# When weights are converted and inner-layer sums are split in the attention half of an attention and mixer kernel

## The chip, the core and the metric

The kernel runs on one core of a Trainium2 chip. The metric is the device time of one execution in microseconds (us): 847.35 as the median of three runs of the kernel before (846.75 to 847.96).

## What is computed

```python
scores = scale * np.matmul(q, k.transpose(0, 1, 3, 2))
mask = (rel >= 0) & (rel < window)
scores = np.where(mask, scores, -1000000000.0)
attn = softmax(scores)
x = concat_heads(np.matmul(attn, v))
xt = x.transpose(0, 2, 1)
h = np.maximum(xt @ w_tok1, 0.0) @ w_tok2
u = x + h.transpose(0, 2, 1)
h2 = np.maximum(u @ w_ch1, 0.0) @ w_ch2
return (u + h2).astype(np.float32)
```

Eight batches of eight heads, 576 tokens, 64 columns a head, a window of 64 tokens. The token layers go 576 to 256 to 576 (w_tok1, w_tok2), the channel layers 512 to 1536 to 512 (w_ch1, w_ch2). The weights come as float64, and every product is made with float32 numbers split into a rounded high part and a low rest, as three matmuls (high by high, high by low, low by high).

## The kernel before

The attention half runs over 36 tiles (two blocks of 64 tokens each; nine tiles make two batches). The loop `for i in range(-1, NT + 1)` is written out as a software pipeline, and every engine does its instructions in the order in which the loop's body issues them: nothing reorders them. "Tile i" below is the stretch in which step i of this loop runs. In it, in TensorE's order:

- `pt_transpose(i, 0)` and `(i, 1)`: the exponentials of tile i (e, two halves u of four heads) are transposed (pp, L311); ScalarE copies the result to SBUF (pt, L313).
- `run_pieces`: up to two pieces of the second token layer (`tok2`, up, L403 and L410), from tile 7 on; ScalarE copies each out (u, L415) before the next can use the one bank.
- `tok1(n)`: the first token layer (h, L368) for the tile before; it needs that tile's x split into xhi (ScalarE, L101) and xlo (GpSimd, L104). The fifth tile of a pair of batches, x4, x13 and so on, is split by halves (L348, L349).
- `av(i, pts)`: probabilities by v (xp, L323).
- `qk(i + 2)`: scores two tiles ahead (s, L276). For the first seven tiles (`N_PE = 7`) TensorE adds the mask (L270), and ScalarE takes the exponentials from PSUM.

VectorE has, per tile: the maxima of tile i+1 by halves (L290 and L291 in tiles below 7, otherwise the mask and scale into e, L293, and the maximum, L296), the reciprocal of the sums (ri, L331 and L332), and the normalisation of tile i (x, L337). ScalarE has eight exponentials per tile (L304).

Two kinds of work are put between these:

- A **weight job** turns one piece of the float64 weights into float32 and splits it. `job_convert_a` is three VectorE operations (L195, L197, L198), `job_convert_b` three more (L207, L209, L210) and a GpSimd addition (w, L212). `job_finish`, one tile later, is a ScalarE cast (t1hi, t2hi or w1hi, L101) and a subtraction (L104): on GpSimd for w_tok1 (t1lo) and w_ch1 (w1lo), on VectorE for w_tok2 (t2lo). `JOBS[i]` says whether tile i converts a piece: tiles -1 to 5, then two of three. 27 pieces are done in this half; jobs 4, 5 and 6 are w_tok2.
- `finish_h(b)`, the **inner-layer split**: when a batch's h is summed up (in tiles 5, 9, 14, 18, 23, ...), ScalarE takes its relu (hhi, L379), VectorE the low rest (hlo, L380). h has two PSUM banks, so the next batch's first h matmul waits until hlo has read the bank.

The channel half (from about 265 us) is matmuls over the token chunks, with Strassen-like products in its larger part; the change issues nothing else there.

Of the kernel before, what the change touches and what calls it, by code (L numbers as in the profile page):

```python
# [26 lines left out]
TPP = 9  # L27
NT = NPAIR * TPP
# [11 lines left out]
N_FIRST = 27  # L40


JOBS = {i: 1 if i < 6 or i % 3 else 0 for i in range(-1, 37)}
PIECES = {32: (1, 0), 33: (1, 0), 34: (1, 0), 35: (3, 0), 36: (2, 1)}

TOK1_FROM, TOK1_SLOW, TOK2_FROM = 2, 4, 7
# [1 line left out]
N_PE, N_EARLY = 7, 4  # L48
# [35 lines left out]
def mixer_kernel(ctx: ExitStack, tc: tile.TileContext, qh, kh, vh, wt1, wt2, wc1, wc2, out):  # L84
# [14 lines left out]
    def split(eng_hi, eng_lo, hi, lo, src):  # L99
        if eng_hi is nc.scalar:  # L100
            nc.scalar.copy(hi, src)  # L101
        else:
            eng_hi.tensor_copy(hi, src)
        eng_lo.tensor_sub(lo, src, hi.bitcast(F32))  # L104
# [18 lines left out]
    with ExitStack() as actx:  # L123
# [21 lines left out]
        def load_v(i):  # L145
            vt = pq.tile([P, 2, H, D], F32, name=f"v{i}", tag="v", bufs=3)
            nc.sync.dma_start(vt, vh[i])
            loaded[i][1] = vt
# [71 lines left out]
        to_load, to_convert, to_finish = list(range(N_FIRST)), [], []  # L220
# [23 lines left out]
        def job_finish():  # L244
            if to_finish:
                n, w = to_finish.pop(0)
                finished.add(n)
                src, hi, lo, o, m = jobs[n]
                if hi is None:
                    nc.sync.dma_start(w2_dram[:, o:o + m], w)  # L250
                else:
                    eng = nc.vector if src is wt2 or n >= N_FIRST else nc.gpsimd
                    split(nc.scalar, eng, hi[:, o:o + m], lo[:, o:o + m], w)
                    if src is wt1 and o + m == 5 * DT:
                        for c, r in enumerate((top, bottom)):
                            nc.gpsimd.tensor_copy(t1z[r, c], t1lo[r, 4 * DT:].bitcast(F32))
# [41 lines left out]
        def softmax_exp(i, u):  # L298
            e = e_sb[i, u]
            nm, sm = st[i]  # L300
            src, by = (s_ps.pop((i, u)), scale) if i < N_PE else (e, 1.0)
            for h in range(4):
                g = 2 * h + u
                nc.scalar.activation(e[:, h], src[:, h], AF.Exp, bias=nm[:, g:g + 1], scale=by,  # L304
                                     accum_out=sm[:, g:g + 1])
# [36 lines left out]
        def split_x(i):  # L342
            xhi = pa.tile([P, C], F32R, name=f"xhi{i}", tag="xhi", bufs=NX)
            xlo = pa.tile([P, C], F32R, name=f"xlo{i}", tag="xlo", bufs=NX)
            if i % TPP == 4:

                for t, own, other in ((xhi, top, bottom), (xlo, bottom, top)):
                    nc.scalar.copy(t[own], xs[i][own])  # L348
                    nc.gpsimd.tensor_sub(t[other], xs[i][own], t[own].bitcast(F32))  # L349
            else:  # L350
                split(nc.scalar, nc.gpsimd, xhi, xlo, xs[i])
            xhl[i] = (xhi, xlo)
# [3 lines left out]
        def tok1_part(i, b, rows, slot, first, last):  # L356
            xhi, xlo = xhl[i]
            if first:
                h_ps[b] = [ps.tile([P, C], F32, name=f"h{b}_{tt}", tag="h") for tt in range(NTT)]
            for tt in range(NTT):  # L360
                if rows is full:
                    combos = ((t1hi, xhi), (t1hi, xlo), (t1lo, xhi))
                else:
                    x = xhi if rows is top else xlo
                    combos = ((t1hi, x), (None, x))
                for n, (w, x) in enumerate(combos):
                    w, o = (t1z[:, rows is bottom], 0) if w is None else (w, slot * DT)
                    nc.tensor.matmul(h_ps[b][tt], w[:, o + tt * P:o + (tt + 1) * P], x,  # L368
                                     start=first and n == 0, stop=last and n == len(combos) - 1)

        pieces, up_tags = [], [("up", 1)]

        def finish_h(b):
            hh = []
            for tt in range(NTT):
                hp = h_ps[b][tt]
                hi = pa.tile([P, C], F32R, name=f"hhi{b}_{tt}", tag=f"hhi{tt}", bufs=2)
                lo = pa.tile([P, C], F32R, name=f"hlo{b}_{tt}", tag=f"hlo{tt}", bufs=2)
                nc.scalar.activation(hi, hp, AF.Relu)  # L379
                nc.vector.scalar_tensor_tensor(out=lo, in0=hp, scalar=0.0, in1=hi.bitcast(F32),  # L380
                                               op0=ALU.max, op1=ALU.subtract)
                hh.append((hi, lo))
            h_ps.pop(b)
            for half in range(2):
                for ct in range(NCT):
                    pieces.append((b, half, ct, hh))
# [46 lines left out]
        def tok1(i):  # L433
            p, t = divmod(i, TPP)
            b0, b1 = 2 * p, 2 * p + 1
            if t < 4:
                tok1_part(i, b0, full, t, t == 0, False)
            elif t == 4:
                tok1_part(i, b0, top, 4, False, True)
                finish_h(b0)  # L440
            else:
                if t == 5:
                    tok1_part(i - 1, b1, bottom, 4, True, False)
                tok1_part(i, b1, full, t - 5, False, t == 8)
                if t == 8:
                    finish_h(b1)

        def run_pieces(k):
            for _ in range(min(k, len(pieces))):
                tok2(*pieces.pop(0))  # L450
# [21 lines left out]
        for i in range(-1, NT + 1):  # L472
            if 0 <= i and i + 2 < NT:
                load_v(i + 2)
            if 3 <= i + 3 < NT:
                load_q(i + 3)
            if i + 4 < NT:
                load_k(i + 4)
            store_u()
            n_jobs = JOBS[i]  # L480
            if i == NT - 1:
                up_tags += [("s", 2), ("pt", 2)]
            have = len(pieces)
            n_pieces = PIECES.get(i, (1, 1) if i >= TOK2_FROM else (0, 0))
            pts = []
            early = i < N_EARLY
            if 0 <= i < NT:
                pts.append(pt_transpose(i, 0))
                if i < NT - 1:
                    pts.append(pt_transpose(i, 1))  # L490
            if i + 1 < NT:
                softmax(i + 1, 0)
            if early and i > 0:
                norm(*normed.pop())
            if 0 <= i < NT:
                ri = recip(i)
            while to_finish:
                job_finish()
            for n in tok1_plan.get(i + 1, ()):
                last_use = n - NX + ((n - NX) % TPP == 4)  # L500
                if n < i and last_use not in tok1_plan.get(i, ()):
                    split_x(n)
            if i + 1 < NT:
                softmax_exp(i + 1, 0)
            run_pieces(min(have, n_pieces[0]))
            have = min(have, len(pieces))
            if not early:
                for _ in range(n_jobs):
                    job_convert_a()
            if i == NT - 1:  # L510
                pts.append(pt_transpose(i, 1))
            if i + 1 < NT:
                softmax(i + 1, 1)
            if early:
                for _ in range(n_jobs):
                    job_convert_a()
            for n in tok1_plan.get(i, ()):
                tok1(n)
            if i + 1 < NT:
                softmax_exp(i + 1, 1)  # L520
            for _ in range(n_jobs):
                job_convert_b()
            if 0 <= i < NT:
                xp = av(i, pts)
                if i + 1 < N_EARLY:
                    normed = [(i, xp, ri)]
                else:
                    norm(i, xp, ri)
            if i + 2 < NT:
                qk(i + 2)  # L530
            for n in tok1_plan.get(i + 1, ()):
                if n not in xhl:
                    split_x(n)
            run_pieces(min(have, n_pieces[1]))
            while to_load and len(to_convert) < 2 and i < NT - 2:
                job_load()
            if i == NT - 1:
                while to_convert or to_convert_b or to_finish:
                    job_convert_a()
                    job_convert_b()  # L540
                    job_finish()
                qctx.close()
                pu = uctx.enter_context(tc.tile_pool(name="pu", bufs=1, side="right", reuse_waits="tile"))
                ul = {0: load_u(0, pu)}
# [396 lines left out]
```

## Time and profile before

| what | value |
|---|---|
| median of three runs | 847.35 us |
| the profiled execution | 847.25 us, its span 845.5 us |
| TensorE busy with matmuls | 817.7 us of the span |
| VectorE, ScalarE, GpSimd busy | 527.6, 338.9, 103.1 us |
| mean granted TensorE clock | 0.998 of full speed |

The span is the time from the first to the last instruction of the profiled execution; 1.75 us lie around it. A matmul's busy time is its own, so neighbours overlap; what counts for the time is where TensorE sits idle, and what ended each such wait.

### The profile page before, as it was taken

The numbers are of one execution on the slowest core, as the hardware profiler recorded it, in microseconds if no ns is written. First come the engines' busy times: TensorE is split into PE (matmuls) and PEld (weight loads), VectorE is DVE, ScalarE is ACT, GpSimd is POOL, SyncE is SP. The second block draws the span as 40 slices with busy tenths as digits, with TensorE's granted clock in tenths as the row PEclk, the third lists the DMA queues.
The fourth block names the chain that finished last, engine by engine and source line by source line (L and its number), as shares of the span: only waits on it lengthen the run. The fifth ranks groups of instructions, "written<-read, shape, count | busy, mean of one in ns | idle before, by whom it ended". The sixth has DMA issues, their size and how long they took to land.

```text
span 845.5 us, 14791 instructions
## 1 busy us (share of the span) xinstructions
PE 817.7 (97%) x5864; PEld 680.1 (80%) x5864; DVE 527.6 (62%) x939; ACT 338.9 (40%) x1018; POOL 103.1 (12%) x109
## 2 busy tenths in 40 slices
PE   6889999999999999999999999999999999999998
PEld 4668878878879878888888888888888878888886
DVE  4989888888885697567415535366635367625252
ACT  4778889889885341213203211123202033202020
POOL 3533343343332000000000000000000000000000
PEclk9999999999999999999999999999999999999999
DMA  9657677677634545745322652424542424542002
GB/s 320 217 182 254 202 238 250 220 232 248 209 132 151 156 149 169 223 137 155 120 93 78 244 227 77 147 88 137 187 187 88 136 88 163 170 178 88 1 0 100
DMA packets 71333, 136.10 MB, mean 161 GB/s; under 512 B 7008, under 2 KB 41568, under 8 KB 69344
## 3 DMA queue, kind: packets, MB, share of 16 engines
q1 hardware_dynamic: 69152, 133.32, 46.6%
q10 hardware_dynamic: 2112, 1.84, 0.7%
q8 instruction: 46, 0.75, 0.4%
q14 instruction: 23, 0.19, 0.1%
HBM read 104.46 MB, written 30.67 MB: 160 GB/s over the span
## 4 chain that ended last, share of the span: by engine, by line
PE 74%; DVE 19%; ACT 2%; issue 2%; DMA 1%; POOL 1%; POOLq 0%; SPq 0%; DVEq 0%; ACTq 0%
PE gp L840 18%; PE op L628 11%; PE gp L620 8%; PE op_4a L628 4%; PE op_2b L628 4%; PE op_2a L628 4%; PE op_0b L628 4%; PE op_0a L628 4%; PE op_4b L628 4%; PE h L368 3%; PE up L410 3%; PE s L276 3%; PE xp L323 2%; DVE nm L296 2%; DVE e L293 2%
## 5 line engine op out<-in xcount | busy, mean ns | idle before, releaser
L840 PE MATMUL gp<-m,w1hi 128*128 128x512 f32 x504 | 155.4, 390 | 0.7 <-DVE x L848 0.7
L840 PEld LDWEIGHTS gp<-m,w1hi 128*128 128x128 f32 x504 | 94.5, 188 | 21.0 <-DVE x L848 1.5
L840 PE MATMUL gp<-m,w1lo 128*128 128x512 f32 x252 | 98.1, 389 | 0.0
L304 ACT ACTIVATE e<-e,nm 128x128 f32<-128x128 f32 x232 | 90.6, 398 | 9.1 <-DVE nm L296 9.0
L607 ACT ACTIVATE ghi<-x 128x512 fp32r<-128x512 f32 x54 | 34.1, 632 | 119.9 <-DVE x L850 68.3
L844 ACT COPY x<-gp 128x512 f32<-128x512 f32 x18 | 10.4, 577 | 143.3 <-PE gp L840 143.3
L608 DVE SCALAR_TENSOR_TENSOR glo<-x,ghi 128x512 fp32r<-128x512 f32 x54 | 37.4, 692 | 38.1 <-ACT ghi L607 38.1
L607 ACT ACTIVATE ghi<-gp 128x512 fp32r<-128x512 f32 x50 | 29.8, 597 | 67.7 <-PE gp L620 67.7
L620 PE MATMUL gp<-uhi,w1hi 128*128 128x512 f32 x144 | 56.0, 389 | 0.0
L620 PE MATMUL gp<-ulo,w1hi 128*128 128x512 f32 x144 | 56.0, 389 | 0.0
L620 PE MATMUL gp<-uhi,w1lo 128*128 128x512 f32 x144 | 56.0, 389 | 0.0
L840 PEld LDWEIGHTS gp<-m,w1lo 128*128 128x128 f32 x252 | 47.3, 188 | 9.9
L608 DVE SCALAR_TENSOR_TENSOR glo<-gp,ghi 128x512 fp32r<-128x512 f32 x50 | 34.3, 687 | 25.4 <-ACT ghi L607 25.3
L628 PE MATMUL op<-ghi,w2hi 128*128 128x512 f32 x128 | 49.8, 389 | 0.0
L628 PE MATMUL op<-ghi,w2lo 128*128 128x512 f32 x128 | 49.8, 389 | 0.0
L628 PE MATMUL op<-glo,w2hi 128*128 128x512 f32 x128 | 49.8, 389 | 0.0
L276 PE MATMUL s<-k,q 64*64 64x128 f32 x1152 | 44.7, 284 | 4.7 <-DVE c L207 2.5
L323 PEld LDWEIGHTS xp<-v,pt 128*64 128x64 f32 x1152 | 37.2, 140 | 13.7 <-issue 7.2
L104 POOL TENSOR_TENSOR xlo<-x,xhi 128x512 fp32r<-128x512 f32 x32 | 41.2, 1286 | 41.0 <-ACT xhi L101 40.6
L304 ACT ACTIVATION_READ_ACCUMULATOR e<-e,nm 128x1 f32 x232 | 45.1, 194 | 0.0
L410 PE MATMUL up<-t2hi,hhi 128*128 128x320 f32 (+1 forms) x128 | 43.0, 336 | 0.0
L323 PE MATMUL xp<-v,pt 128*64 128x64 f32 x1152 | 42.1, 227 | 0.8 <-ACT pt L313 0.6
(165 smaller groups left out, 1881.8 us busy)
## 6 DMA issues: line engine op xcount, KB each, us to landing
v<-vh SPq DMA_DIRECT2D x36, 512.0 KB, 3.9
w1hi<-w1s SPq DMA_DIRECT2D x18, 896.0 KB, 4.8
w1lo<-w1s SPq DMA_DIRECT2D x18, 896.0 KB, 6.6
raw<-wc SPq DMA_DIRECT2D x32, 384.0 KB, 4.3
q<-qh SPq DMA_DIRECT2D x36, 256.0 KB, 4.6
k<-kh SPq DMA_DIRECT2D x7, 1280.0 KB, 7.5
out<-uf SPq DMA_DIRECT2D x35, 256.0 KB, 2.6
uf<-u_dram SPq DMA_DIRECT2D x8, 1024.0 KB, 8.7
```

What stands on the lines that cost most here:

```text
L104: eng_lo.tensor_sub(lo, src, hi.bitcast(F32))
L276: nc.tensor.matmul(s[u][half * BLK:(half + 1) * BLK, j], qt[r, j, half], kbs[b][r, j, n * BLK:n * BLK + P], start=not on_pe, stop=True, sk ...
L293: nc.vector.scalar_tensor_tensor(out=e, in0=s_ps.pop((i, u)), scalar=scale, in1=mk.unsqueeze(1).to_broadcast([P, 4, P]), op0=ALU.mult, op1 ...
L304: nc.scalar.activation(e[:, h], src[:, h], AF.Exp, bias=nm[:, g:g + 1], scale=by, accum_out=sm[:, g:g + 1])
L323: nc.tensor.matmul(xp[half * BLK:(half + 1) * BLK, h], pts[h % 2][:, h // 2, half * BLK:(half + 1) * BLK], vt[:, half, h], start=True, sto ...
L368: nc.tensor.matmul(h_ps[b][tt], w[:, o + tt * P:o + (tt + 1) * P], x, start=first and n == 0, stop=last and n == len(combos) - 1)
L410: nc.tensor.matmul(up[:, :n], hx[:, cs], w[:, tt * S + s0:tt * S + s0 + n], start=False, stop=(k == 6), skip_group_check=True)
L607: nc.scalar.activation(hi, src, AF.Relu)
L608: nc.vector.scalar_tensor_tensor(out=lo, in0=src, scalar=0.0, in1=hi.bitcast(F32), op0=ALU.max, op1=ALU.subtract)
L620: nc.tensor.matmul(gp, w[:, w1_at(ft, ct)], x[:, ct], start=(k == 0), stop=(k == 3 * NCT - 1))
L628: nc.tensor.matmul(op, w[:, ct, ft], x[:, cols], start=(first and k == 0), stop=(last and k == 3 * len(gs) - 1), skip_group_check=not (fir ...
L840: nc.tensor.matmul(b, w[:, at], c[:, h, t], start=(n < 4 and k == 0), stop=(k == 5), skip_group_check=True)
```

## The change

It does four things. Weight jobs after tile 5 go to the tiles whose number modulo 9 is not 0, 3 or 5, so tiles 14, 23 and 32, which split an inner layer, convert nothing, tiles 6, 15, 24 and 33 do, and the last piece is converted in tile 34, not 35. In the tiles below 7 `job_finish` goes behind the second half's exponentials, and `job_convert_a` behind the second half's maxima (before, this was so only below tile 4). The first half's exponentials go ahead of the early `split_x`. And `finish_h` of the one split below tile 7, that of batch 0 in tile 5, goes behind the normalisation and the split of x5.

```diff
--- before.py
+++ after.py
@@ -40,7 +40,7 @@
 N_FIRST = 27
 
 
-JOBS = {i: 1 if i < 6 or i % 3 else 0 for i in range(-1, 37)}
+JOBS = {i: 1 if i < 6 or i % TPP not in (0, 3, 5) else 0 for i in range(-1, 37)}
 PIECES = {32: (1, 0), 33: (1, 0), 34: (1, 0), 35: (3, 0), 36: (2, 1)}
 
 TOK1_FROM, TOK1_SLOW, TOK2_FROM = 2, 4, 7
@@ -371,6 +371,7 @@
         pieces, up_tags = [], [("up", 1)]
 
         def finish_h(b):
+
             hh = []
             for tt in range(NTT):
                 hp = h_ps[b][tt]
@@ -437,13 +438,19 @@
                 tok1_part(i, b0, full, t, t == 0, False)
             elif t == 4:
                 tok1_part(i, b0, top, 4, False, True)
-                finish_h(b0)
+                done.append(b0)
             else:
                 if t == 5:
                     tok1_part(i - 1, b1, bottom, 4, True, False)
                 tok1_part(i, b1, full, t - 5, False, t == 8)
                 if t == 8:
-                    finish_h(b1)
+                    done.append(b1)
+
+        done = []
+
+        def finish_done():
+            while done:
+                finish_h(done.pop())
 
         def run_pieces(k):
             for _ in range(min(k, len(pieces))):
@@ -494,30 +501,36 @@
                 norm(*normed.pop())
             if 0 <= i < NT:
                 ri = recip(i)
-            while to_finish:
-                job_finish()
+            if i >= N_PE:
+                while to_finish:
+                    job_finish()
+            if i + 1 < NT:
+                softmax_exp(i + 1, 0)
             for n in tok1_plan.get(i + 1, ()):
                 last_use = n - NX + ((n - NX) % TPP == 4)
                 if n < i and last_use not in tok1_plan.get(i, ()):
                     split_x(n)
-            if i + 1 < NT:
-                softmax_exp(i + 1, 0)
             run_pieces(min(have, n_pieces[0]))
             have = min(have, len(pieces))
-            if not early:
+            if i >= N_PE:
                 for _ in range(n_jobs):
                     job_convert_a()
             if i == NT - 1:
                 pts.append(pt_transpose(i, 1))
             if i + 1 < NT:
                 softmax(i + 1, 1)
-            if early:
+            if i < N_PE:
                 for _ in range(n_jobs):
                     job_convert_a()
             for n in tok1_plan.get(i, ()):
                 tok1(n)
+            if i >= N_PE:
+                finish_done()
             if i + 1 < NT:
                 softmax_exp(i + 1, 1)
+            if i < N_PE:
+                while to_finish:
+                    job_finish()
             for _ in range(n_jobs):
                 job_convert_b()
             if 0 <= i < NT:
@@ -531,6 +544,7 @@
             for n in tok1_plan.get(i + 1, ()):
                 if n not in xhl:
                     split_x(n)
+            finish_done()
             run_pieces(min(have, n_pieces[1]))
             while to_load and len(to_convert) < 2 and i < NT - 2:
                 job_load()
```

TensorE's order is the same instruction for instruction. Three places where the other engines' order moves, as the built programs have it. Line numbers from 374 on are one to fourteen higher in the changed kernel; the numbers behind the names are those of buffers.

ScalarE from tile 5's second copy of transposed probabilities (pt_1) to tile 6's first, before:

```order
L313 COPY pt_1_746<-pp_1_741 128x512
L101 CAST t2hi<-w_676 128x384
L304 ACTIVATE e_0_750,sum_749<-s_0_700,nm_748 128x128 x4
L379 ACTIVATE hhi_0_773<-h_0_455 128x512
L379 ACTIVATE hhi_1_777<-h_1_456 128x512
L304 ACTIVATE e_1_766,sum_749<-s_1_702,nm_748 128x128 x4
L101 CAST xhi_828<-x_808 128x512
L313 COPY pt_0_843<-pp_0_838 128x512
```

and now:

```order
L313 COPY pt_1_746<-pp_1_741 128x512
L304 ACTIVATE e_0_750,sum_749<-s_0_700,nm_748 128x128 x4
L304 ACTIVATE e_1_760,sum_749<-s_1_702,nm_748 128x128 x4
L101 CAST t2hi<-w_676 128x384
L101 CAST xhi_820<-x_800 128x512
L380 ACTIVATE hhi_0_824<-h_0_453 128x512
L380 ACTIVATE hhi_1_828<-h_1_454 128x512
L313 COPY pt_0_843<-pp_0_838 128x512
```

The cast t2hi and the two inner-layer relus hhi stood ahead of exponentials and of xhi (the high part of x5); now the cast stands behind both halves' exponentials, and the relus behind the cast and xhi.

VectorE in tile 6, from the mask and scale of tile 7's first half to the normalisation of tile 6 (x), before:

```order
L293 SCALAR_TENSOR_TENSOR e_0_854<-s_0_810,mask_90 128x512
L296 TENSOR_REDUCE nm_852<-e_0_854 128x4
L331 TENSOR_SCALAR ri_857<-sum_749 128x8
L332 RECIPROCAL ri_857<-ri_857 128x8
L104 TENSOR_TENSOR t2lo<-w_786,t2hi 128x384
L293 SCALAR_TENSOR_TENSOR e_1_866<-s_1_811,mask_90 128x512
L296 TENSOR_REDUCE nm_852<-e_1_866 128x4
L337 TENSOR_TENSOR x_902<-xp_885,ri_857 128x512
```

and now:

```order
L331 TENSOR_SCALAR ri_857<-sum_749 128x8
L332 RECIPROCAL ri_857<-ri_857 128x8
L293 SCALAR_TENSOR_TENSOR e_1_864<-s_1_803,mask_90 128x512
L296 TENSOR_REDUCE nm_852<-e_1_864 128x4
L195 TENSOR_SCALAR c_867<-raw_726 128x384
L197 TENSOR_SCALAR c_867<-c_867 128x384
L198 TENSOR_SCALAR c_867<-c_867 128x384
L104 TENSOR_TENSOR t2lo<-w_778,t2hi 128x384
L207 SCALAR_TENSOR_TENSOR c_867<-raw_726,c_867 128x384
L209 TENSOR_SCALAR r_889<-c_867 128x384
L210 SCALAR_TENSOR_TENSOR r_889<-raw_726,r_889 128x384
L337 TENSOR_TENSOR x_912<-xp_895,ri_857 128x512
```

(the first row here is the reciprocal; the two rows ahead of it are the same as before). The normalisation stood right behind the second maxima; now six conversions of a weight job and the subtraction t2lo, which was ahead of the second half, stand between.

VectorE in tile 14, an inner-layer split, from the first maxima to the normalisation, before:

```order
L332 RECIPROCAL ri_1775<-ri_1775 128x8
L195 TENSOR_SCALAR c_1795<-raw_1520 128x384
L197 TENSOR_SCALAR c_1795<-c_1795 128x384
L198 TENSOR_SCALAR c_1795<-c_1795 128x384
L293 SCALAR_TENSOR_TENSOR e_1_1799<-s_1_1714,mask_90 128x512
L296 TENSOR_REDUCE nm_1770<-e_1_1799 128x4
L380 SCALAR_TENSOR_TENSOR hlo_0_1807<-h_0_1329,hhi_0_1806 128x512
L380 SCALAR_TENSOR_TENSOR hlo_1_1811<-h_1_1330,hhi_1_1810 128x512
L207 SCALAR_TENSOR_TENSOR c_1795<-raw_1520,c_1795 128x384
L209 TENSOR_SCALAR r_1818<-c_1795 128x384
L210 SCALAR_TENSOR_TENSOR r_1818<-raw_1520,r_1818 128x384
L337 TENSOR_TENSOR x_1841<-xp_1824,ri_1775 128x512
```

and now:

```order
L332 RECIPROCAL ri_1789<-ri_1789 128x8
L293 SCALAR_TENSOR_TENSOR e_1_1809<-s_1_1728,mask_90 128x512
L296 TENSOR_REDUCE nm_1784<-e_1_1809 128x4
L381 SCALAR_TENSOR_TENSOR hlo_0_1817<-h_0_1343,hhi_0_1816 128x512
L381 SCALAR_TENSOR_TENSOR hlo_1_1821<-h_1_1344,hhi_1_1820 128x512
L337 TENSOR_TENSOR x_1845<-xp_1828,ri_1789 128x512
```

The six conversion rows (L195 to L210) are gone from this tile; tile 15 now has them. Tiles 23 and 32 read alike.

## Rows read from the trace of the kernel before

**Rows 1.** The page's first part: busy us, share, instructions.

```profile
PE 817.7 (97%) x5864; PEld 680.1 (80%) x5864; DVE 527.6 (62%) x939; ACT 338.9 (40%) x1018; POOL 103.1 (12%) x109
```

**Rows 2.** Windows: busy of PE, PEld, DVE, ACT, POOL; clock; DMA; GB/s.

```profile
13.90:61.50 47.60, 39.72 (x555) 30.40 (x552) 40.30 (x90) 36.17 (x143) 18.95 (x19) 0.96 0.64 228
...
54.40:58.00 3.60, 3.60 (x17) 3.15 (x14) 3.46 (x8) 2.76 (x8) 2.27 (x2) 0.54 0.07 25
...
110.00:125.00 15.00, 13.20 (x184) 11.10 (x183) 12.24 (x21) 12.27 (x45) 5.70 (x7) 1.00 0.71 232
...
172.00:188.00 16.00, 14.09 (x193) 10.89 (x186) 13.88 (x23) 13.34 (x46) 7.33 (x8) 1.00 0.79 252
...
235.00:250.00 15.00, 13.81 (x188) 10.70 (x181) 13.01 (x23) 12.49 (x44) 4.97 (x5) 1.00 0.56 186
```

**Rows 3.** TensorE's timeline: start, us, line, operation, count, [idle <- releaser].

```profile
53.44 1.09 PE L276 MATMUL s<-k,q 64*64 64x128 f32 x28 [2.52 <-DVE c L207]
...
118.94 0.44 PE L403 MATMUL up<-ident,x 128*128 128x128 f32 x2 [1.70 <-ACT u L415]
...
183.82 0.50 PE L368 MATMUL h<-xlo,t1hi 128*128 128x512 f32 x1 [0.85 <-POOL xlo L104]
```

**Rows 4.** Timeline: normalisations of tiles 3 to 6; a later h matmul.

```profile
38.88 0.68 DVE L337 TENSOR_TENSOR x<-xp,ri 128x512 f32<-128x512 f32 x1
...
45.41 0.68 DVE L337 TENSOR_TENSOR x<-xp,ri 128x512 f32<-128x512 f32 x1
...
54.35 0.68 DVE L337 TENSOR_TENSOR x<-xp,ri 128x512 f32<-128x512 f32 x1
...
60.60 0.69 DVE L337 TENSOR_TENSOR x<-xp,ri 128x512 f32<-128x512 f32 x1 [1.35 <-PE xp L323]
...
63.62 0.40 PE L368 MATMUL h<-xlo,t1hi 128*128 128x512 f32 x1
```

**Rows 5.** Timeline of ScalarE and VectorE, tiles 4 and 5.

```profile
39.59 0.62 ACT L101 CAST xhi<-x 128x512 fp32r<-128x512 f32 x1 [2.23 <-DVE x L337]
...
40.12 1.06 ACT L313 COPY pt<-pp 128x512 f32<-128x512 f32 x2
...
41.07 0.52 ACT L101 CAST t2hi<-w 128x384 fp32r<-128x384 f32 x1
...
41.63 0.56 DVE L104 TENSOR_TENSOR t2lo<-w,t2hi 128x384 fp32r<-128x384 f32 x1 [0.96 <-ACT t2hi L101]
...
43.95 0.55 DVE L207 SCALAR_TENSOR_TENSOR c<-raw,c 128x384 int32<-128x384 int32 x1
...
47.41 1.07 ACT L313 COPY pt<-pp 128x512 f32<-128x512 f32 x2
...
48.93 0.36 ACT L304 ACTIVATE e<-s,nm 128x128 f32<-128x128 f32 x1
...
50.31 1.09 ACT L379 ACTIVATE hhi<-h 128x512 fp32r<-128x512 f32 x2
...
51.70 1.28 DVE L380 SCALAR_TENSOR_TENSOR hlo<-h,hhi 128x512 fp32r<-128x512 f32 x2
```

**Rows 6.** Groups by line: busy us, mean ns, idle before, releaser.

```profile
L304 ACT ACTIVATE e<-e,nm 128x128 f32<-128x128 f32 x232 | 90.6, 398 | 9.1 <-DVE nm L296 9.0
...
L296 DVE TENSOR_REDUCE nm<-e 128x4 f32<-128x512 f32 x58 | 39.8, 686 | 2.0
...
L293 DVE SCALAR_TENSOR_TENSOR e<-s,mask 128x512 f32<-128x512 f32 x58 | 39.3, 677 | 3.0 <-PE s L276 3.0
```

**Rows 7.** Timeline of tile 2: GpSimd subtraction, small VectorE operation.

```profile
28.61 1.27 POOL L104 TENSOR_TENSOR xlo<-x,xhi 128x512 fp32r<-128x512 f32 x1
...
28.74 1.17 DVE L291 TENSOR_SCALAR nm<-nm 128x4 f32<-128x4 f32 x1
```

**Rows 8.** Timeline: tile 14's normalisation; tile 24's second exponentials.

```profile
117.23 0.68 DVE L337 TENSOR_TENSOR x<-xp,ri 128x512 f32<-128x512 f32 x1
...
178.54 0.40 ACT L304 ACTIVATE e<-e,nm 128x128 f32<-128x128 f32 x1 [0.27 <-DVE nm L296]
```

## The prediction

> **What bounds the kernel now.** First the page's shares: TensorE is busy 817.7 us of the span's 845.5 [rows 1], so nothing can give back more than the 27.8 us in which it sits idle. TensorE's instructions stand in the same order after the change; only its waits can move. So the next view is TensorE's timeline, row by row for idle time: after the opening the long waits lie in tiles 4 to 6 and around tiles 14, 23 and 32. The longest is 2.52 us in tile 5, before scores that need the exponentials of tile 6 out of PSUM [rows 3]. The windows show what follows it: 3.60 us at a granted clock of 0.54, that is about the lower of its two levels, 1.2 GHz, after TensorE had waited 2.52 us and worked one more; 3.60 x 0.46 = 1.7 us are lost there [rows 2].
>
> The third view is VectorE's and ScalarE's timeline in the same tiles. VectorE is busy 40.30 of the 47.60 us from tile 0 to tile 6 [rows 2], and the normalisations x3, x4, x5 and x6 pace the tiles: they start at 38.88, 45.41, 54.35 and 60.60 [rows 4]. The h matmul of tile 7 needs the split of x6 and comes at 63.62, 3.02 us after x6 began [rows 4]. So the change's cost or gain in the opening is read from when x6 comes.
>
> **The change, tiles 3 to 6.** I lay out the new queues between one normalisation and the next, with the starts of the old rows as pitches. The common links, from [rows 5]: normalisation to its ScalarE cast 0.71 (38.88 to 39.59); cast to the copies pt 0.53; the pair of copies 0.95; four exponentials from PSUM 1.38 (48.93 to 50.31); t2hi to t2lo 0.56; t2lo itself 0.56; job_convert_b up to the normalisation 1.46 (43.95 to 45.41).
>
> - x3 to x4: before 6.53. Now t2hi stands behind both halves' exponentials, t2lo waits for it, and the conversions and x4 are queued behind t2lo on VectorE. 0.71 + 0.53 + 0.95 + 2 x 1.38 + 0.56 + 0.56 + 1.46 = 7.53: 1.00 later.
> - x4 to x5: before 8.94. The copies of tile 5 start 2.00 after x4 (47.41), then 0.95 + 2.76 + 0.56 + 0.56 + 1.46: in all 8.29, 0.65 earlier. What goes here is the relu between the exponentials and VectorE's wait for t2hi ahead of the maxima, so the 2.52 wait shrinks. What is late next is hlo.
> - x5 to x6: before 6.25. Three things now stand between. The inner-layer split is behind x5: 0.71 to xhi, 0.53 to hhi, half of 1.09 for the first hhi, 1.28 for both hlo, 3.07 in all [rows 5], before VectorE can begin tile 6. Then two rounds of mask and maximum at 0.68 and 0.69 [rows 6], with some 0.36 between them for the reciprocal (an estimate: two operations on eight columns), 3.10; four exponentials at 0.40, 1.59 [rows 6]; then t2hi 0.56, t2lo 0.56 and, new in tile 6, a weight job's 1.46. The other three conversions lie beside the exponentials and cost nothing; without that cover they would add about as much again. In all 3.07 + 3.10 + 1.59 + 2.58 = 10.34: 4.09 later.
>
> Together x6 comes 1.00 - 0.65 + 4.09 = **4.4 us later**, and the h matmul of tile 7 with it. The wait moves there: TensorE idles before the first h of the next batch, whose bank hlo must have read, and before h of tile 7. From there VectorE's order is as before, so TensorE, which cannot run faster than its rows, keeps the delay.
>
> **Tiles 0 to 3.** The casts t1hi leave the exponentials' way. The nearest row of a moved cast is 0.52 [rows 5], and it can count once, because behind it VectorE paces the tiles: -0.5 at best. Against it, the order of GpSimd's work turns. In tile 2 a VectorE operation on four columns takes 1.17 us while a GpSimd subtraction runs, and ends with it [rows 7]; about 1.0 of that is waiting. I count one such meeting in each of tiles 1 to 3 as it is now. Now the two GpSimd subtractions of a tile (xlo, then t1lo) both fall among the six conversions. If they stretch one operation a tile as now, the cost is -0.5; if one more in each of three tiles, +2.5. I take **+0.6**, nearer the low end, because one stretch partly replaces another.
>
> The Trainium skill, page "SBUF — State Buffer", section "Who interferes with whom", has it that whichever of GpSimd and a VectorE operation in a two-port mode issues first holds the shared port for the whole instruction, and the other blocks fully. By that rule taken strictly every conversion begun under a subtraction waits, and the sum below would be 1.9 higher; by the row's count of one a tile, 1.1 lower. The row in tile 2 agrees that the wait is a full one; how many there will be it cannot show.
>
> **Tiles 14, 23, 32 and after.** Without the six conversions x14 (117.23 [rows 8]) can follow hlo directly, at least the 1.46 of job_convert_b sooner. ScalarE's copy of a piece, behind xhi, comes sooner too, and that ends the wait of 1.70 at 118.94 [rows 3]. All that TensorE idles in these stretches is 15.00 - 13.20 = 1.80, 16.00 - 14.09 = 1.91 and 15.00 - 13.81 = 1.19 [rows 2], 4.9 together: the upper end. Not all of it comes back. In tile 24 the second exponentials waited only 0.27 for VectorE [rows 8], the rest of the time for the relus and the first half on ScalarE, so the transposes come 0.27 earlier and no more; to this comes the 0.85 for xlo [rows 3], 1.1 in all. And tiles 15, 24 and 33 now convert, with a stretch of up to 1.0 as in [rows 7]: the lower ends are 0.7, 0.1 and 0.1, 0.9 together. I take 1.4, 0.8 and 0.6, nearer to the waits' own rows, **-2.8**. The last piece's conversion leaves tile 35, where TensorE has other pieces to do: nothing.
>
> The DMA queue's order changes with it (some pieces are loaded a tile sooner). I cost that at nothing, because each load is still issued at least a tile ahead of its conversion, whose six operations it would otherwise hold up on VectorE.
>
> **Sum**, against the profiled execution's 847.25, which is 0.1 from the median of 847.35: +4.4 + 0.6 - 2.8 = +2.2, **849.4 us**. With all low ends (-0.5, 4.9) it is 846.2, with all high ends (+2.5, 0.9) 853.2. About 0.2%, 1.7 us, is what a measurement can tell from no change.
>
> **The rivals.**
>
> - **Faster: the opening runs free.** The order that puts softmax first takes these stretches of 1.0 out of tiles 1 to 3, as nothing of GpSimd meets an operation that needs the port. Then tiles 0 to 3 give -3.5 instead of +0.6, and 847.25 - 3.5 + 4.4 - 2.8 = 845.3. It decides once 2.8 of the 3.0 us of stretches go. For it: such a stretch needs the two operations to meet, and their order is turned. Against: GpSimd has as many operations as before. 0.25.
> - **Nothing to tell.** The three splits give back their whole idle time, 4.9: 847.3, the gain and the delay of x6 even out. For it: the six conversions are the largest thing between these waits and their causes. Against: the 0.27. 0.23.
> - **Slower, by the port.** Two stretches a tile, +2.5: 851.3. For it: both subtractions now fall among the conversions. Against: a conversion that comes first may hold GpSimd back instead. The rule of the Trainium skill's page "SBUF — State Buffer" would have it so where the subtraction comes first. 0.10.
> - **Slower, by the clock.** TensorE now idles about 3 us before the next batch's h (the 3.07 above), and again before h of tile 7. The row at 0.54 came after 2.52 us of idle [rows 2, 3]. If the lower level falls on h of tile 7, where TensorE is late itself, another 1.7 us: 851.1. 0.07.
> - My forecast: 0.35, of which 0.05 ends within 0.2%.
>
> **How the numbers follow.** Slower 0.30 + 0.10 + 0.07 = 0.47; same 0.23 + 0.05 = 0.28; faster 0.25. The forecast's own range is 846.2 to 853.2. For eight in ten the range reaches down to 844.8, past the faster case's 845.3, and leaves out the part of it in which late gains add to it.
>
> **What would show it.** Right: x6 starts near 65 us (60.60 + 4.4 + 0.6 = 65.6), with hlo of batch 0 behind x5 and TensorE idle for some 3 us before the next batch's first h; h of tile 7 waits for xlo of x6, near 68.6. The 2.52 wait before scores in tile 5 is below 1. Tile 14's wait of 1.70 is gone, tile 24's transposes come little earlier relative to tile 23's. Wrong: x6 at or before 62, VectorE's operations in tiles 1 to 3 without times above 1 us, or new waits on VectorE in tiles 15, 24 and 33 that eat the late gain.

## The result, and the profile after

The changed kernel takes 850.73 us (median of 5 runs, 850.59 to 851.54), the kernel before 847.35 beside it: a ratio of 1.0041, interval 1.0031 to 1.0052. It is slower, by 3.4 us; 849.4 was forecast. The profiled execution took 851.32 us, 4.07 more than the one before, its span 849.4.

The page's first part, changed kernel, answers to [rows 1]: no engine has more work to speak of.

```profile
PE 818.4 (96%) x5864; PEld 681.1 (80%) x5864; DVE 527.4 (62%) x939; ACT 337.4 (40%) x1018; POOL 103.6 (12%) x109
```

So the time went into waits, and the normalisations tell where. The changed kernel's VectorE timeline, x3 to x7, answers to [rows 4]:

```profile
39.79 0.68 DVE L337 TENSOR_TENSOR x<-xp,ri 128x512 f32<-128x512 f32 x1
...
47.26 0.68 DVE L337 TENSOR_TENSOR x<-xp,ri 128x512 f32<-128x512 f32 x1
...
55.62 0.68 DVE L337 TENSOR_TENSOR x<-xp,ri 128x512 f32<-128x512 f32 x1
...
65.80 0.68 DVE L337 TENSOR_TENSOR x<-xp,ri 128x512 f32<-128x512 f32 x1
...
73.38 0.68 DVE L337 TENSOR_TENSOR x<-xp,ri 128x512 f32<-128x512 f32 x1
```

x6 was forecast at 65.6 and came at 65.80. Read from the start of one normalisation to the next, each minus the same step before, the whole opening and the late places stand in one table; the last two columns are the first and third experiment below.

| step (us) | forecast | changed kernel | jobs alone | order alone |
|---|---|---|---|---|
| x0 to x3 | +0.6 | +1.16 | +0.03 | +1.17 |
| x3 to x4 | +1.00 | +0.94 | +0.01 | +0.94 |
| x4 to x5 | -0.65 | -0.58 | 0.00 | -0.57 |
| x5 to x6 | +4.09 | +3.93 | +1.89 | +2.48 |
| x6 to x7 | 0 | +0.90 | +0.92 | -0.03 |
| x7 to x13 | 0 | +0.01 | +0.01 | +0.01 |
| x13 to x22 (tile 14) | -1.4 | -1.87 | -1.87 | +0.01 |
| x22 to x31 (tile 23) | -0.8 | -0.05 | +0.02 | +0.01 |
| x31 to x35 (tile 32) | -0.6 | -0.23 | -0.23 | +0.04 |
| sum | +2.2 | +4.21 | +0.78 | +4.06 |

(x0 itself came 0.25 earlier than before, and so x35 3.96 later; with the jobs alone x0 came 0.69 earlier, with the order alone 0.18.) The profiled execution shows 4; the median, 3.4, lies a little below it.

TensorE's timeline of the changed kernel, answering to [rows 3] (last the idle time before the matmul and what ended it):

```profile
50.05 0.50 PE L368 MATMUL h<-xhi,t1hi 128*128 128x512 f32 x1 [2.31 <-POOL xhi L349]
58.33 0.77 PE L368 MATMUL h<-xlo,t1hi 128*128 128x512 f32 x1 [2.34 <-POOL xlo L104]
...
67.19 0.50 PE L368 MATMUL h<-xhi,t1hi 128*128 128x512 f32 x1 [0.86 <-ACT xhi L101]
68.54 0.50 PE L368 MATMUL h<-xlo,t1hi 128*128 128x512 f32 x1 [0.85 <-POOL xlo L104]
...
182.96 1.48 PE L311 MATMUL pp<-ident,e 128*128 128x128 f32 x4 [0.60 <-ACT e L304]
...
199.15 0.55 PE L404 MATMUL up<-ident,x 128*128 128x128 f32 x3 [0.73 <-ACT u L416]
...
206.66 0.55 PE L404 MATMUL up<-ident,x 128*128 128x128 f32 x3 [0.35 <-ACT u L416]
```

The 2.52 before tile 5's scores [rows 3] is gone; 2.31 before x4's half (1.37 before) and 2.34 before the next batch's first h stand in its place. The row at 58.33 names xlo, but that matmul reads the half of x4, which was split by 51.4; by the order of the instructions it waits for the bank that hlo reads late. At tile 23 the old 0.85 is gone, and so is an idle time that TensorE had there before:

```profile
177.78 1.09 PE L276 MATMUL s<-k,q 64*64 64x128 f32 x28 [0.92 <-DVE e L293]
```

The 0.60, 0.73 and 0.35 are new, the last two of them two and three tiles later: 1.68 for 1.77.

The windows, answering to [rows 2] (busy time of PE, PEld, DVE, ACT and POOL, clock, DMA share, GB/s):

```profile
57.00:62.00 5.00, 3.67 (x10) 2.86 (x10) 4.37 (x10) 3.71 (x13) 1.27 (x1) 0.66 0.22 76
62.00:70.00 8.00, 6.29 (x90) 4.84 (x90) 6.67 (x13) 5.32 (x22) 3.29 (x3) 1.00 0.48 151
114.00:129.00 15.00, 14.91 (x203) 13.00 (x199) 12.21 (x24) 13.28 (x47) 6.32 (x6) 1.00 0.80 268
176.00:192.00 16.00, 15.23 (x214) 12.45 (x207) 12.98 (x26) 13.53 (x47) 6.93 (x7) 1.00 0.85 286
239.00:255.00 16.00, 15.15 (x205) 12.16 (x196) 13.39 (x26) 13.59 (x47) 6.23 (x6) 1.00 0.44 148
```

A low clock (0.66 from 57 to 62) lies in tile 6, and another (0.51 from 51.0 to 54.5) in tile 5; in both the chain of ScalarE and VectorE sets the pace, not TensorE. Tile 7 has the full clock.

### The profile page after: what moved, and what is told of

The parts are those of the page before. It is cut to its first block, busy times and chain, and to the rows that moved or that the text cites. A ratio compares the mean times of both kernels' runs of the same rounds, so it can differ in the third digit from the quotient of the medians.

```text
span 849.4 us, 14799 instructions
## 1 busy us (share of the span) xinstructions
PE 818.4 (96%) x5864; PEld 681.1 (80%) x5864; DVE 527.4 (62%) x939; ACT 337.4 (40%) x1018; POOL 103.6 (12%) x109
## 3 DMA queue, kind: packets, MB, share of 16 engines
q10 hardware_dynamic: 2112, 1.84, 0.7%
## 4 chain that ended last, share of the span: by engine, by line
PE 72%; DVE 19%; ACT 5%; issue 2%; DMA 1%; POOLq 0%; POOL 0%; SPq 0%; DVEq 0%; ACTq 0%
PE gp L854 18%; PE op L642 11%; PE gp L634 8%; PE op_4a L642 4%; PE op_2b L642 4%; PE op_2a L642 4%; PE op_0b L642 4%; PE op_0a L642 4%; PE op_4b L642 4%; PE up L411 3%; PE h L368 2%; ACT e L304 2%; PE s L276 2%; DVE nm L296 2%; DVE e L293 2%
```

## The experiments

Each ratio is to runs of the kernel before that were made beside it, whose medians were 848.08 to 848.78 us. Times of different experiments are therefore compared by these ratios.

**The two halves of the change.** First the table of conversions alone, in the order of before:

```diff
-JOBS = {i: 1 if i < 6 or i % 3 else 0 for i in range(-1, 37)}
+JOBS = {i: 1 if i < 6 or i % TPP not in (0, 3, 5) else 0 for i in range(-1, 37)}
```

> The kernel before with the new table of weight jobs and nothing else (tile 6 converts a piece, tiles 14, 23 and 32 don't). Theory A (the opening's delay is a serial chain made by the new order of casts, exponentials and inner-layer split, and the piece in tile 6 is a part of it): x6 waited 1.35 us for TensorE before, so a piece's 2.6 us on VectorE makes x6 about 1.2 later, its finishing in tile 7 another 0.9; the later tiles give back 2.1: 847.4 us. Theory B (the piece in tile 6 alone makes the opening's 6.1 us, the order is harmless): 847.35 + 6.1 - 2.1 = 851.3 us.

Measured: 847.32 us, ratio 0.9998 (0.9987 to 1.0008). Then the same without the conversion in tile 6:

```diff
+JOBS = {i: 1 if i < 6 or i > 6 and i % TPP not in (0, 3, 5) else 0 for i in range(-1, 37)}
```

> The kernel before with only the later weight jobs moved (from tiles 14, 23, 32 to 15, 24, 33; none in tile 6). Theory A: x4 to x6 start as in the kernel before, the later tiles give back about 2.1 us as in the changed kernel: 845.2 us. Rival (the conversions only carry their wait one tile on; what the changed kernel got back later it got because it was late): 847.3 us.

Measured: 846.27 us, ratio 0.9974 (0.9964 to 0.9984). And the new order with the old table:

```diff
-JOBS = {i: 1 if i < 6 or i % TPP not in (0, 3, 5) else 0 for i in range(-1, 37)}
+JOBS = {i: 1 if i < 6 or i % 3 else 0 for i in range(-1, 37)}
```

> The changed kernel with the old table of weight jobs: the order alone. Theory A: x6 is 5.2 less 1.5 (the conversions ahead of it in tile 6) = 3.7 us later than before, nothing is given back later: 851.0 us. Theory B (order harmless): 847.3 us.

Measured: 852.3 us, ratio 1.0046 (1.0033 to 1.0058). The order alone costs about 4 us. The table alone comes to nothing: it gives about 2 back at tile 14 and loses 2.8 in tiles 6 and 7, through the one conversion that tile 6 gains (2.1 was expected; the ratios of these first two runs lie 2.0 us apart). In the second run x5 to x7 take as long as before, and all of the late gain stays.

**Where the order costs.** The inner-layer split back ahead of the second exponentials in every tile, the rest as changed:

```diff
-            if i >= N_PE:
-                finish_done()
+            finish_done()
```

> The changed kernel with the inner-layer split of tile 5 in its old place, ahead of the second half's exponentials. Theory A: x5 comes about 1.1 later (two relus ahead of the exponentials and the cast on ScalarE), but tile 6's mask follows x5 by 0.6 and not by 3.1: 1.4 us less in all, 849.3 us. Rival (the split is hidden, as TensorE has nothing to do there anyway): 850.7 us.

Measured: 851.66 us, ratio 1.0034 (1.0021 to 1.0047). The medians do not tell it from the changed kernel; the normalisations do: x4 to x5 is 0.97 longer than in the changed kernel, x5 to x6 1.84 shorter, 0.87 less in all, where 1.4 was expected. The late split is a cost, but of 0.9: about half of what it puts between x5 and x6 it takes from between x4 and x5. This profile also lost about 1.7 us to a low clock near 320 us, for which see the end.

Then the finishing of a piece (t2hi, t2lo) back ahead of the exponentials in tiles 4 to 6 (`if i >= N_EARLY` at the first place of job_finish, `if i < N_EARLY` at the second):

> The changed kernel, but in tiles 4 to 6 the finishing of a converted weight piece (t2hi on ScalarE, t2lo on VectorE) stands ahead of the exponentials again, as before. Theory A (t2hi behind eight exponentials is what delays x4 and x6): in the changed kernel the step from x3 to x4 grew by 0.94, the one from x4 to x5 shrank by 0.58, the one from x5 to x6 grew by 3.93 us. With the finishing back, the 0.94 goes, the 0.58 goes with it, and x6 comes 1.0 to 1.6 earlier than in the changed kernel, because VectorE's last conversions follow the maxima at once instead of t2lo. The time is then 849.1 to 849.7 where the kernel before takes 847.35 (ratio 1.002 to 1.003). Theory B (the exponentials set the pace whatever stands around them): x6 within 0.3 us of the changed kernel's, ratio 1.004.

Measured: 849.39 us, ratio 1.0015 (1.0006 to 1.0025). VectorE's timeline of this run, x3 to x6:

```profile
39.69 0.68 DVE L337 TENSOR_TENSOR x<-xp,ri 128x512 f32<-128x512 f32 x1
...
46.35 0.69 DVE L337 TENSOR_TENSOR x<-xp,ri 128x512 f32<-128x512 f32 x1
...
54.33 0.69 DVE L337 TENSOR_TENSOR x<-xp,ri 128x512 f32<-128x512 f32 x1
...
63.42 0.69 DVE L337 TENSOR_TENSOR x<-xp,ri 128x512 f32<-128x512 f32 x1
```

x3 to x4 takes 6.66, nearly the 6.53 of before; x4 to x5 7.98; x5 to x6 9.09 against 10.18 in the changed kernel. From x3 to x6 that is 2.28 less, more than theory A gave. A was wrong in one thing: it took the 0.58 between x4 and x5 for a gain of the late finishing. It grew to 0.96 without it, and the run before lost it with the late split, so it belongs to the late split. In this run the clock is 0.84 over 40 to 70 us, and still x7 comes 2.4 earlier than in the changed kernel: TensorE's clock did not set the pace there.

**The opening tiles.** GpSimd's t1lo left out (its tile is filled with zeros, so the low part of the first inner weight is missing from the result):

```diff
-                    split(nc.scalar, eng, hi[:, o:o + m], lo[:, o:o + m], w)
+                    if src is wt1:
+                        nc.scalar.copy(hi[:, o:o + m], w)
+                    else:
+                        split(nc.scalar, eng, hi[:, o:o + m], lo[:, o:o + m], w)
```

> The changed kernel without GpSimd's subtraction that makes t1lo, the low part of the first inner weight; t1lo is filled with zeros at the start, so the low part of that weight is left out of the result. Theory A (a VectorE conversion that meets this subtraction waits it out, and that wait is on the path): the three stretched conversions of 1.02, 0.81 and 0.85 us in tiles 1 to 3 return to 0.36, and the stretch from x0 to x3, 19.34 us in the changed kernel and 18.18 before, becomes about 17.7. Theory B (the stretches lie beside ScalarE's exponentials and cost nothing; the opening tiles are later because the casts t1hi now stand behind them): 19.1 to 19.4 us. The rest of the program is unchanged, so the span becomes about 1.6 us shorter under A and stays under B.

Measured: 848.87 us in one run, span 846.9. VectorE's timeline of the changed kernel: the six stretched conversions between x0 and x3, two a tile:

```profile
23.34 1.45 DVE L207 SCALAR_TENSOR_TENSOR c<-raw,c 128x320 int32<-128x320 int32 x1
24.90 1.02 DVE L209 TENSOR_SCALAR r<-c 128x320 int32<-128x320 int32 x1
...
29.70 1.35 DVE L198 TENSOR_SCALAR c<-c 128x320 int32<-128x320 int32 x1
...
31.68 0.81 DVE L209 TENSOR_SCALAR r<-c 128x320 int32<-128x320 int32 x1
...
36.34 1.31 DVE L198 TENSOR_SCALAR c<-c 128x384 int32<-128x384 int32 x1
...
38.35 0.85 DVE L209 TENSOR_SCALAR r<-c 128x384 int32<-128x384 int32 x1
```

GpSimd's timeline of the same kernel, its two subtractions in tile 1; the two conversions begin under them and end behind them:

```profile
23.11 1.34 POOL L104 TENSOR_TENSOR xlo<-x,xhi 128x512 fp32r<-128x512 f32 x1 [1.78 <-ACT xhi L101]
24.86 0.87 POOL L104 TENSOR_TENSOR t1lo<-w,t1hi 128x320 fp32r<-128x320 f32 x1 [0.41 <-ACT t1hi L101]
```

And of the run without t1lo, x0 and x3, and the three that are left (line numbers here are 1 to 4 higher):

```profile
19.79 0.69 DVE L341 TENSOR_TENSOR x<-xp,ri 128x512 f32<-128x512 f32 x1
...
23.13 1.21 DVE L210 TENSOR_SCALAR r<-c 128x320 int32<-128x320 int32 x1
...
28.22 1.35 DVE L199 TENSOR_SCALAR c<-c 128x320 int32<-128x320 int32 x1
...
34.45 1.32 DVE L199 TENSOR_SCALAR c<-c 128x384 int32<-128x384 int32 x1
...
37.42 0.68 DVE L341 TENSOR_TENSOR x<-xp,ri 128x512 f32<-128x512 f32 x1
```

x0 to x3 takes 17.63 us: theory A's 17.7. (The span is 2.5 shorter; 1.71 comes from here, 0.66 from an earlier x0.) The sum closes better than that. Add up, for every VectorE operation between x0 and x3, its time above the shortest of its form in these traces, and take that from the stretch: before 18.18 - 4.15 = 14.03, changed 19.34 - 5.30 = 14.04, without t1lo 17.63 - 3.61 = 14.02. VectorE's own work, with the short gaps in it, is the same 14.03 in all three. What lies above it is the whole difference, and all but about 0.1 us of it falls on operations that overlap one of GpSimd's. The Trainium skill, page "SBUF — State Buffer", section "Who interferes with whom", says that an instruction of VectorE with two SBUF inputs also contends with a GpSimd instruction that reads SBUF; L207 at 1.45 us, 0.49 where nothing runs beside it, agrees.

**The late places.** One conversion moved from tile 14 to 15, in the kernel before:

```diff
+JOBS = {i: 1 if i < 6 or i % 3 else 0 for i in range(-1, 37)} | {14: 0, 15: 1}
```

> The kernel before with one conversion moved from tile 14 to tile 15 and nothing else. Theory A (of the three late places only the first gives something lasting, as the normalisations of the second experiment say: -1.9 us at tile 14, 0.0 at tile 23, -0.2 at tile 32): 1.7 to 2.0 us less than the kernel before, ratio 0.9977 to 0.998. Theory B (my prediction's 1.4, 0.8 and 0.6): 1.4 us less, ratio 0.9983, and x27 of the profile 0.8 us later than in the second experiment, relative to x22.

Measured: 845.34 us, ratio 0.9971 (0.996 to 0.9982). The interval holds A's ratio and just misses B's; the normalisations decide: from x13 to x35 this run gains 1.81 us, the second run with all three places 2.09, and x22 to x27 is as before in both, to 0.02. Tile 14 brings nearly all of it.

Could tile 23's conversion go elsewhere? Both runs have the move at tile 14 and the sooner split of the next paragraph:

```diff
+JOBS = {i: 1 if i < 6 or i % 3 else 0 for i in range(-1, 37)} | {14: 0, 15: 1, 23: 0, 27: 1}
```

> The kernel before with one conversion moved from tile 14 to 15, one from tile 23 to 27 (no longer to 24), and the last returned piece of the second weight split one inner tile sooner. With the move to tile 24, the idle of 0.92 and 0.85 us around tile 23 turned into 0.60 before a transpose, 0.73 and 0.35 before up for ScalarE's u in tiles 25 and 26. Theory A (the waits for u come from the converting tiles 24, 25 and 26 right behind the split, where TensorE has no backlog): without a conversion in tile 24, 25 and 26 are as before; the idle of 1.8 shrinks to 0.6 to 0.7 and nothing is given back, so the normalisations from x28 on stand 1.0 to 1.2 earlier relative to x22 than before, and the time is 842.5 to 843.4 where the kernel before takes 847.35 (ratio 0.9943 to 0.9953). Theory B (ScalarE's or VectorE's sum of work over these tiles sets the pace, wherever the conversion goes): the same time is given back in tiles 27 to 29; ratio 0.9956 to 0.9965.

Measured: 845.05 us, ratio 0.9958 (0.9946 to 0.9971). And with `18: 1` in the place of `27: 1`:

> As the run before it, but the conversion of tile 23 goes to tile 18, so that tiles 15 to 20 convert in a row, ahead of the split instead of behind it. Theory A: there TensorE has a backlog or not as the rows show; in tiles 15 to 17 three converting tiles in a row brought no wait. If none appears in tiles 18 to 20, the gain at tile 23 stays: x28 1.0 to 1.2 earlier relative to x17 than before, ratio 0.9943 to 0.9953. Theory B (a row of converting tiles brings waits for u wherever it stands): waits of 0.3 to 0.7 before up in tiles 18 to 21, which give back 1 us or more: ratio 0.9956 to 0.997.

Measured: 845.54 us, ratio 0.9963 (0.995 to 0.9977). TensorE's timeline, in order the run with tile 27 and the run with tile 18:

```profile
206.95 0.44 PE L403 MATMUL up<-ident,x 128*128 128x128 f32 x2 [1.03 <-ACT u L415]
214.41 0.44 PE L403 MATMUL up<-ident,x 128*128 128x128 f32 x2 [0.72 <-ACT u L415]
```

```profile
146.82 0.44 PE L403 MATMUL up<-ident,x 128*128 128x128 f32 x2 [1.56 <-ACT u L415]
154.28 0.44 PE L403 MATMUL up<-ident,x 128*128 128x128 f32 x2 [0.72 <-ACT u L415]
```

Theory A falls in both: x28 stands 0.49 later relative to x22 than before in the one, and in the other x16 to x28 grew by 0.87. What the conversion gives where it is absent is real: x22 to x26 takes 1.82 us less than before in the run with tile 27, and x22 to x31 takes 1.82 less in the run with tile 18. But it takes more than that back where it goes: 2.31 in tiles 27 and 28 of the one; in tiles 18 to 22 of the other, 2.84 against the run with tile 14 alone.

The price can be read from the pitch of the tiles without a split. In the kernel before, tiles 8, 20 and 29, which finish a piece and convert the next, take 7.46 to 7.48 us. Tiles 11, 17 and 26 do the same two things in 6.73 or 6.74, as long as tile 10, which only converts (6.73). VectorE's and GpSimd's timeline of before, tile 8 and then tile 17, shows what differs:

```profile
70.35 1.02 POOL L104 TENSOR_TENSOR w1lo<-w,w1hi 128x384 fp32r<-128x384 f32 x1 [0.37 <-ACT w1hi L101]
...
70.50 1.08 DVE L197 TENSOR_SCALAR c<-c 128x384 f32<-128x384 f32 x1
```

```profile
133.47 0.36 DVE L197 TENSOR_SCALAR c<-c 128x384 f32<-128x384 f32 x1
...
133.87 0.36 DVE L198 TENSOR_SCALAR c<-c 128x384 int32<-128x384 int32 x1
```

In tile 8 a conversion begins 0.15 behind the subtraction w1lo and waits it out; in tile 17 w1lo begins at 134.08, when the last of the first three conversions has begun, and nothing is stretched. All tiles of this kind in the traces of before and of the changed kernel keep to this: 7.45 to 7.58 us with a stretched conversion (1.06 to 1.16), 6.73 or 6.74 without. The 0.73 between tiles 8 and 17 is what L197 takes longer (1.08 for 0.36). In the changed kernel the conversion in tile 24 makes tile 25 finish as well; tiles 25 and 26 both have a stretched conversion and take 7.47 and 7.45, where they took 6.75 and 6.74. Behind tile 14 only tile 17 gets one. New ones in the two runs here are tile 28 with the move to 27, and tile 19 with the move to 18: 7.52 each, 6.73 before.

**A version that beats both.** The second run, with one more edit in the channel half: the last of the three pieces of the second weight that come back from memory is split one inner tile sooner.

```diff
-            if ft in (6, 8, 10):
+            if ft in (6, 8, 9):
```

> The kernel before with the conversions moved in the late tiles alone (the second experiment), and with the last of the three pieces of the second weight that come back from memory split one inner tile sooner, before the tenth relu instead of after. In all kernels so far TensorE waits 1.7 to 2.1 us for this piece near 313 to 319 us; in three of the six profiles the granted clock falls to 0.56 to 0.6 for some 3.5 us after that wait, and those spans are 1.5 us longer than the normalisations alone would make them. Theory A (the wait is real and nothing else is late behind it): 1.8 us less than the second experiment, and the profiles with a low clock there are gone, so the median falls by 1.8 to 3.4: ratio to the kernel before 0.9935 to 0.9955. Theory B (VectorE is the bound there, and the next piece is late instead): ratio 0.997 as in the second experiment.

Measured: 844.38 us, ratio 0.9956 (0.9941 to 0.997), span 842.2. The wait near 313 us fell from 1.83 to 0.51, now for glox, a new wait that A had not named. From x35 to the span's end this run takes 583.3 us, the kernels with the old split and a full clock there 584.5 to 584.7: 1.2 to 1.4 less, not the 1.8 of A. The ratio lies just above A's range and its interval reaches B's 0.997; it is the trace that speaks for A, with a smaller gain. The run's interval and that of the run with tile 27 overlap almost wholly. Nothing of the new order is in it.

## Why the prediction came out as it did

The side and the mechanism were right. That x6 was placed to 0.2 us is partly luck: tiles 0 to 3 cost 0.56 more than forecast, tiles 3 to 6 cost 0.15 less, and x0 came 0.25 earlier. The sum came out 2.0 too low in the profiled execution (4.21 for 2.24), by three terms (0.90, 0.56 and 0.65, less 0.15 in tiles 3 to 6).

- **Tiles 3 to 6, right.** +1.00, -0.65 and +4.09 against +0.94, -0.58 and +3.93. The jobs and the order alone split the last: 2.48 by the order, and with both 1.45 more, the 1.46 that was taken for tile 6's conversion. That t2lo's place costs was shown (2.28 from x3 to x6 with the finishing back). The split's 3.07 was its length in the new place; as a cost of moving it, 0.87 was measured. The h matmul of tile 7 that waits for xlo came at 68.54 for 68.6, but the idle time before the next batch's h was 2.34, not some 3.
- **"From there VectorE's order is as before": wrong, 0.90.** The piece that tile 6 now converts is finished in tile 7. ScalarE casts it ahead of the exponentials, GpSimd subtracts, and VectorE's first conversion waits that out. The changed kernel's rows of ScalarE, GpSimd and VectorE, and VectorE's row of before:

```profile
67.99 0.52 ACT L101 CAST w1hi<-w 128x384 fp32r<-128x384 f32 x1
...
68.59 1.02 POOL L104 TENSOR_TENSOR w1lo<-w,w1hi 128x384 fp32r<-128x384 f32 x1
...
68.66 1.16 DVE L195 TENSOR_SCALAR c<-raw 128x384 int32<-128x384 int32 x1
```

```profile
63.49 0.31 DVE L195 TENSOR_SCALAR c<-raw 128x384 int32<-128x384 int32 x1
```

  The same operation took 0.31 in tile 7 before; 0.85 of the 0.90 is in this row. With the jobs alone the step is +0.92, without tile 6's conversion 0. A job was costed by the tile that it is moved into and not by the one that finishes it.
- **Tiles 0 to 3: +0.6 against +1.16.** The casts' -0.5 did not come: 14.03 us of VectorE's work are left whatever ScalarE does. The stretched operations did, as the rival had it, two a tile (six, 4.59 us above their own time, for four and 3.33; the forecast had counted three). But the second of a tile waits only 0.5 to 0.7, so the rival's +2.5 was too much, and the forecast's term too little.
- **Late places: -2.8 against -2.1.** Tile 14 gave 1.87 (1.4 forecast). Tile 23's 0.8 was the idle time in one window, and it came back in tile 24 and two tiles on as waits for u. Tile 32 gave 0.2 of 0.6: a wait of 0.85 for xlo is still there, one tile later. The reservation that "tiles 15, 24 and 33 now convert" was the right one for tile 23: its low end of 0.1 is what came. So a sign that the prediction had named for being wrong, new waits in these tiles that eat the gain, came true at this one of the three places, though the waits were for ScalarE and not for VectorE.
- **The clock: no part in the result.** The rival wanted the low level on tile 7, which had 1.00. The wait of 2.52 went, low clocks came in tiles 5 and 6, and the chain of ScalarE and VectorE hid them: the order alone had 1.00 from 50 to 70 us, the same steps from x3 to x5, and from x5 to x6 only the 1.45 less that tile 6's conversion accounts for. In the order of before the clock does count. The run with the sooner split does the same instructions up to x7 and has the same wait of 2.52 us, but its granted clock was 0.50 from 52 to 58 us, where before has 0.72. Its x5 and x6:

```profile
53.36 0.68 DVE L337 TENSOR_TENSOR x<-xp,ri 128x512 f32<-128x512 f32 x1
...
60.80 0.69 DVE L337 TENSOR_TENSOR x<-xp,ri 128x512 f32<-128x512 f32 x1 [1.48 <-PE xp L323]
```

  That is 7.44 us for 6.25 (the late jobs alone, 0.72 in the same window: 6.27), with x6 waiting for TensorE each time. So there is such a cost, as the prediction argued, though no run shows its 1.7; the longer low stretch cost 1.2 here. The change could not gain by it, because x6 no longer waits for TensorE.
- **The rivals.** "Opening runs free" needed stretches to vanish; there are more. "Even out" needed 4.9 from the late places, which gave 2.1. The port's 851.3 and the clock's 851.1 lie nearer to the measured time than the forecast, but by luck: the port's 2.5 measured 1.16, the low level did not fall on tile 7, and what brings the sum there is tile 7's wait and the late places.

## What to carry to other kernels

Where one in-order engine paces a stretch, write its time as its own work plus what it waits out beside another engine: here the first part was constant to 0.02 us over three kernels, and the second was the whole effect. Cost a piece of work in the tile that finishes it too, and look in the old trace for tiles that already do both: their pitch is the price, and where such tiles differ, look for the operation that is stretched in the longer ones. Idle time beside a split is a gain only if no later tile is paced by the same work: follow the positions a whole period on before counting it.

## What the chip showed besides

All kernels but the three with the sooner split wait 1.7 to 2.1 us for the same weight piece near 313 to 319 us, and what follows differs from one profile to the next. TensorE's timeline and a window of the second experiment:

```profile
312.80 0.50 PE L628 MATMUL op<-ghix,w2lo 128*128 128x512 f32 x1 [1.83 <-DVE w2lo L104]
```

```profile
313.50:317.50 4.00, 4.00 (x13) 3.12 (x12) 3.83 (x10) 0.94 (x2) 0.00 (x0) 0.57 0.31 81
```

The same two of the changed kernel:

```profile
319.14 0.50 PE L642 MATMUL op<-ghix,w2lo 128*128 128x512 f32 x1 [1.89 <-DVE w2lo L104]
```

```profile
320.00:324.00 4.00, 4.00 (x19) 3.32 (x18) 3.86 (x10) 0.98 (x2) 0.00 (x0) 1.00 0.24 61
```

After 1.83 us of idle TensorE's granted clock fell to 0.57, about the lower of its two levels (1.2 GHz), after 1.89 it stayed at the upper; 4.00 x 0.43 = 1.7 us hang on it. Of the nine profiles with this wait three show the low clock (the late jobs, the order alone, the split put back, after 1.83, 1.83 and 2.13 us of idle), and six do not (after 1.67 to 1.89). From x35 to the span's end the three take 586.2 to 586.6 us, the six 584.5 to 584.7. It fits the scatter of single runs of some kernels (844.25 to 847.85 with tile 14 alone), but no run shows that this is what scatters. With the wait at 0.5 us, five runs lie within 1.4 us.
